# Seven block products for the first product of an expert, in a kernel of pooled attention and two mixtures of experts

## The chip, the core and the metric

The kernel runs on one core of one Trainium2 chip, as one program. The metric is the time of one execution on the device in microseconds (us), the median of several runs. A profile of one more execution gives the start and the length of every instruction on the engines: PE (TensorE; PEld is its weight load, which lies beside the matmuls), DVE (VectorE), ACT (ScalarE), POOL (GpSimd) and SP, which here only issues transfers. In the rows of the profile a name ending in q (SPq, PEq) is the engine's instruction sequencer.

## What is computed

An attention over keys and values that are pooled by eight, then a mixture of eight experts of which each token takes two, then a mixture of four experts that every token takes. There are 2304 tokens of 512 numbers; every expert is a product with a 512 by 1024 matrix, a ReLU and a product with a 1024 by 512 matrix. The two mixtures, cut to the core:

```python
for e in range(E):                      # 8 experts, the two best of a token
    for k in range(2):
        mask = top2[:, k] == e
        h = np.maximum(x[mask] @ w1[e], 0.0)
        out[mask] += top2_w[mask, k, None] * (h @ w2[e])
...
for e in range(E):                      # 4 experts, all of them
    h = np.maximum(x @ w1[e], 0.0)
    out += p[:, e:e + 1] * (h @ w2[e])
```

## The kernel before

**Attention and routing** take the first tenth of the time. Tokens stand on the partitions in 18 tiles of 128. Each tile's attention output goes to a DRAM tensor `x_d`; the routing (the generator `routing`, some 60 small DVE operations for a group of tiles, run a few at a time by `step`) turns the noisy logits into lists of tokens for each expert. An expert of the first mixture has 640 slots, that is 5 tiles.

**The first mixture** runs 16 chunks, two for each expert, of 384 and 256 slots. The rows of a chunk are fetched by POOL with an indirect DMA (`gather`, line 490), turned by four PE transposes each and split by ACT and DVE into a rounded part and a remainder (`turn`, lines 497 to 501), because every product is made of three float32r products: rounded times rounded, rounded times remainder, remainder times rounded. `layer1` makes 8 blocks of 128 hidden units for a chunk: 12 matmuls (4 blocks of the depth, 3 terms) into one PSUM bank, with the chunk's tokens as the 384 or 256 columns that stream by (line 593). ACT applies the ReLU (595) and DVE keeps the remainder (596). `layer2` makes 128 tokens by 512 outputs: 24 matmuls of 512 columns into one bank (607). The results go to a DRAM tensor `y_d`.

**The second mixture** takes 18 tiles as six chunks of 384 tokens. A token's two rows of `y_d` are fetched by POOL (`fetch2`), mixed (`mix2`), turned, and stay in SBUF for four experts; three chunks run through expert 0, 1, 2, 3, then the other three through 3, 2, 1, 0.

**The weights** come as 120 transfers of 512 KB (line 467), two blocks of 128 hidden units each. `w_split` rounds them on ACT (475) and takes the remainder on DVE (476); eight slots hold the result. In the attention phase and in the first chunk the remainder is taken by POOL instead, eight times.

**The order of the work** is written out by hand. Each engine runs its queue in the order in which the program text issues the instructions. `run_chunk` counts units (8 of `layer1`, then two for each tile of `layer2`), and `fills` says before which unit a fetch, a mix or a turn is issued. A conditional (line 718, between the last two chunks of the first mixture) holds a slow path for an overfull expert; it isn't taken here, but every engine reads its condition.

Of the kernel before, what the change touches and what calls it, by code (L numbers as in the profile page):

```python
# [29 lines left out]
CHUNKS = ((256, 384),) + ((384, 256),) * (E1 - 1)  # L30
CA = 384
# [9 lines left out]
WP, WP1 = 8, 6  # L41
# [4 lines left out]
def tile_attention_moe_moe(  # L46
# [256 lines left out]
    nc.gpsimd.memset(least[:, 0:1], float(CHUNKS[0][0]))  # L303
# [3 lines left out]
    def routing(g, hold):  # L307
# [99 lines left out]
        if g == EARLY - 1 or last:  # L407
            slots[last] = consts.tile([128, HC], I32, name=f"slots{int(last)}")
            nc.vector.tensor_copy(slots[last], slotf)
            fetch1(int(last))  # L410
            yield
# [38 lines left out]
    seq = [(wa, e) for e in range(E1)]  # L450
    seq += [(wb, e) for e in range(E2)]
    seq += [(wb, e) for e in range(E2 - 2, -1, -1)]
    n_pairs = 8 * len(seq)
    w_sl = [None] * WP
    for i in range(WP1):
        w_sl[i] = wts1.tile([128, 2, 2, 512], FR, name=f"w{i}")
    w_st = {}
    w_at = {"load": 0, "split": 0, "used": 0}

    def w_load():  # L460
        s = w_at["load"]
        if s < n_pairs:
            x, p = divmod(s, 8)
            src, e = seq[x]
            w_st[s] = stg.tile([128, 2, 512], FT, name="w_st")
            j = p % 4
            nc.sync.dma_start(w_st[s], src[e, p // 4][:, 2 * j:2 * j + 2])
            w_at["load"] += 1

    def w_split(eng=None):  # L470
        s = w_at["split"]
        if s >= min(n_pairs, w_at["used"] + WP):
# [7 lines left out]
    def w_get(x, m, f, part):  # L480
        s = 8 * x + 4 * m + f // 2
        assert w_at["used"] <= s < w_at["split"], (x, m, f, w_at)
        return w_sl[s % WP][:, f % 2, part]


    gat, mid, xt = {}, [], []

    def gather(key, src, n, idx):
        g = mid[0].tile([128, DM], FT, name="gat", bufs=6)
# [4 lines left out]
    def turn(src, dst, c):  # L494
# [3 lines left out]
        p3 = p.rearrange("p (k c) -> p k c", c=128)  # L498
        hi = dst[:, 0, :, c * 128:(c + 1) * 128]
        nc.scalar.activation(hi, p3, AF.Copy)  # L500
        nc.vector.tensor_sub(dst[:, 1, :, c * 128:(c + 1) * 128], p3, hi.bitcast(FT))  # L501

    def fetch1(ci):
# [299 lines left out]
```

## Time and profile before

| | before |
|---|---|
| median of three runs | 1390.43 us (1389.38 to 1391.59) |
| the profiled execution | 1388.02 us, of which the span of the instructions is 1386.2 us |
| granted TensorE clock, mean | 0.988 of full speed |
| PE busy | 1358.1 us, 98% of the span |
| DVE, ACT, POOL busy | 504.2, 392.4, 132.3 us |
| DMA | 118.33 MB, a mean of 85 GB/s |

A row of the list by shape names the source line, the engine, the operation, the output and inputs, and then the number of instructions and their busy time; the mean length of a matmul there holds the time until its result has left the array, so that consecutive matmuls overlap, and the spacing of a stream is read from the starts in the timeline. In the list of stretches the columns are the stretch, its length, then for PE, PEld, DVE, ACT and POOL the busy time and the number of instructions, the granted clock, the DMA share and GB/s.

### The profile page before, as it was taken

The numbers are of one execution on the slowest core, as the hardware profiler recorded it, in microseconds if no ns is written. First come the engines' busy times: TensorE is split into PE (matmuls) and PEld (weight loads), VectorE is DVE, ScalarE is ACT, GpSimd is POOL, SyncE is SP. The second block draws the span as 40 slices with busy tenths as digits, with TensorE's granted clock in tenths as the row PEclk, the third lists the DMA queues.
The fourth block names the chain that finished last, engine by engine and source line by source line (L and its number), as shares of the span: only waits on it lengthen the run. The fifth ranks groups of instructions, "written<-read, shape, count | busy, mean of one in ns | idle before, by whom it ended". The sixth has DMA issues, their size and how long they took to land.

```text
span 1386.2 us, 18129 instructions
## 1 busy us (share of the span) xinstructions
PE 1358.1 (98%) x7511; PEld 1238.0 (89%) x7511; DVE 504.2 (36%) x958; ACT 392.4 (28%) x759; POOL 132.3 (10%) x130
## 2 busy tenths in 40 slices
PE   7888999999999999999999999999999999999998
PEld 6787899998999989899999999999999999999997
DVE  6886324342243422433322432323213313313311
ACT  6752334343343433422211222212212212212211
POOL 6422200010000000331000010001000000000000
PEclk9988999999999999999999999999999999999999
DMA  9542423243232422441210310202001101102000
GB/s 369 192 137 64 157 99 124 101 157 114 100 124 99 150 91 85 149 134 46 79 43 16 97 56 31 91 24 69 24 0 58 64 0 61 62 0 61 31 30 24
DMA packets 37896, 118.33 MB, mean 85 GB/s; under 512 B 4784, under 2 KB 6064, under 8 KB 36656
## 3 DMA queue, kind: packets, MB, share of 16 engines
q1 hardware_dynamic: 31728, 97.18, 20.6%
q0 software_dynamic: 6080, 19.93, 4.6%
q8 instruction: 61, 1.00, 0.3%
q14 instruction: 27, 0.22, 0.0%
HBM read 97.17 MB, written 19.92 MB: 84 GB/s over the span
## 4 chain that ended last, share of the span: by engine, by line
PE 59%; issue 0%; ACT 0%; DVE 0%
PE p L593 30%; PE p L607 29%; PE tr L497 1%; DVE acc L738 0%; ACT yo L639 0%; ACT xt L500 0%
## 5 line engine op out<-in xcount | busy, mean ns | idle before, releaser
L593 PE MATMUL p<-xt,w 128*128 128x384 f32 (+1 forms) x3840 | 643.9, 326 | 2.2 <-ACT xt L500 1.5
L593 PEld LDWEIGHTS p<-xt,w 128*128 128x128 f32 x3840 | 631.4, 190 | 6.2 <-ACT xt L500 1.9
L607 PE MATMUL p<-w,hs 128*128 128x512 f32 x2688 | 624.5, 391 | 0.0
L607 PEld LDWEIGHTS p<-w,hs 128*128 128x128 f32 x2688 | 501.7, 188 | 102.2
L595 ACT ACTIVATE hs<-p 128x384 fp32r<-128x384 f32 (+1 forms) x320 | 150.6, 470 | 686.2 <-PE p L593 684.2
L596 DVE SCALAR_TENSOR_TENSOR hs<-p,hs 128x384 fp32r<-128x384 f32 (+1 forms) x320 | 169.0, 529 | 479.4 <-ACT hs L595 479.2
L476 DVE TENSOR_TENSOR w<-w_st,w 128x1024 fp32r<-128x1024 f32 x112 | 137.2, 1225 | 49.0 <-ACT w L475 49.0
L475 ACT ACTIVATE w<-w_st 128x1024 fp32r<-128x1024 f32 x120 | 126.5, 1054 | 1.4 <-DMA w_st<-wb 1.3
L738 DVE SCALAR_TENSOR_TENSOR acc<-p,pe,acc 128x512 f32<-128x512 f32 x54 | 40.6, 751 | 225.7 <-PE p L607 225.7
L490 POOL DMA_INDIRECT gat<-y_d,rows x36 | 41.8, 1160 | 432.8 <-ACT x L653 325.0
L639 ACT ACTIVATE yo<-p 128x512 f32<-128x512 f32 x40 | 23.9, 598 | 172.5 <-PE p L607 167.3
L490 POOL DMA_INDIRECT gat<-x_d,slots x40 | 39.7, 993 | 331.1 <-PE tr L497 285.6
L500 ACT ACTIVATE xt<-tr 128x512 fp32r<-128x512 f32 x58 | 34.4, 596 | 79.1 <-PE tr L497 78.8
L501 DVE TENSOR_TENSOR xt<-tr,xt 128x512 fp32r<-128x512 f32 x58 | 39.9, 689 | 32.7 <-ACT xt L500 32.6
L269 PE MATMUL pv<-va,et 128*128 128x81 f32 (+1 forms) x320 | 40.5, 286 | 5.2 <-DVE lgm L283 5.2
L269 PEld LDWEIGHTS pv<-va,et 128*128 128x128 f32 (+1 forms) x320 | 38.1, 201 | 6.9 <-issue 5.5
L736 DVE TENSOR_SCALAR acc<-p,pe 128x512 f32<-128x512 f32 x18 | 13.5, 751 | 68.7 <-PE p L607 68.7
L231 PE MATMUL s<-kb,q_sb 128*128 128x144 f32 (+1 forms) x160 | 27.9, 319 | 5.8 <-DMA q_sb<-qt 3.1
L231 PEld LDWEIGHTS s<-kb,q_sb 128*128 128x128 f32 (+1 forms) x160 | 21.1, 193 | 8.3 <-issue 4.0
L248 ACT ACTIVATE es<-s,mx 128x72 f32<-128x72 f32 x108 | 25.5, 320 | 10.0 <-DVE mx L238 6.8
L497 PE MATMUL tr<-ident,gat 128*128 128x128 f32 x160 | 24.6, 280 | 1.0 <-DVE xt L501 1.0
L262 ACT ACTIVATE et<-et 72x512 f32<-72x512 f32 x36 | 21.4, 594 | 7.8 <-PE et L260 7.5
(105 smaller groups left out, 320.0 us busy)
## 6 DMA issues: line engine op xcount, KB each, us to landing
w_st<-wa SPq DMA_DIRECT2D x64, 512.0 KB, 4.5
w_st<-wb SPq DMA_DIRECT2D x56, 512.0 KB, 3.9
y_d<-yo SPq DMA_DIRECT2D x40, 256.0 KB, 2.0
x_d<-xs SPq DMA_DIRECT2D x18, 256.0 KB, 4.2
out<-acc SPq DMA_DIRECT2D x18, 256.0 KB, 2.0
k_st<-kt SPq DMA_DIRECT2D x3, 1152.0 KB, 11.4
v_st<-vt SPq DMA_DIRECT2D x3, 1152.0 KB, 11.7
q_sb<-qt SPq DMA_DIRECT2D x3, 1152.0 KB, 14.2
```

Of the source, the lines that this page charges most:

```text
L231: nc.tensor.matmul(p[r0:r1, h * 144:(h + 1) * 144], q_sb[b][:, hp, a0:a1], kb[:, b, hp, :], start=True, stop=True)
L269: nc.tensor.matmul(p[r0:r1, h * VW:(h + 1) * VW], ets[i][:, h * 128 + r0:h * 128 + r1], va[:, b * H + 4 * g + h, :], start=True, stop=True)
L475: nc.scalar.activation(w[:, :, 0], w_st[s], AF.Copy)
L476: (eng or nc.vector).tensor_sub(w[:, :, 1], w_st[s], w[:, :, 0].bitcast(FT))
L490: nc.gpsimd.indirect_dma_start(out=g, out_offset=None, in_=src[0:n, :], in_offset=bass.IndirectOffsetOnAxis(ap=idx, axis=0))
L497: nc.tensor.transpose(p[:, kd * 128:(kd + 1) * 128], src[:, kd * 128:(kd + 1) * 128], ident)
L501: nc.vector.tensor_sub(dst[:, 1, :, c * 128:(c + 1) * 128], p3, hi.bitcast(FT))
L593: nc.tensor.matmul(p, w[:, kd], xs[:, b, kd, :n], start=i == 0, stop=i == 3 * KD - 1)
L595: nc.scalar.activation(hs[:, 0, f, :n], p, AF.Relu)
L596: nc.vector.scalar_tensor_tensor(hs[:, 1, f, :n], p, 0.0, hs[:, 0, f, :n].bitcast(FT), op0=OP.max, op1=OP.subtract)
L607: nc.tensor.matmul(p, hs[:, a, f, t * 128:(t + 1) * 128], w_get(x, 1, f, b), start=f == 0 and i == 0, stop=f == FB - 1 and i == 2)
L738: nc.vector.scalar_tensor_tensor(a, p, w, a, op0=OP.mult, op1=OP.add)
```

## The change

**First product.** Where a chunk is large enough, the product of its tokens with a pair of hidden blocks is made in 2 by 2 blocks (two halves of the tokens by two halves of the depth, two halves of the depth by two hidden blocks) with seven block products and 15 additions instead of eight products (Strassen's scheme in Winograd's form). Each block product has 6 matmuls (2 blocks of the depth, 3 terms). Six experts of the first mixture run so, with all 640 slots as one chunk, hence 320 columns; and in the second mixture the tokens go as three chunks of 768, hence 384 columns, through four experts each, but for the first expert of the first chunk. That one and the first and last experts of the first mixture stay in the plain form (`run_plain`), in pieces of 256 or 384 tokens.

**Sums.** Four sums of token blocks are made by DVE once for a chunk (`sums`), and the seven operands are rounded by ACT (`x_hi`) and their remainders taken by DVE (`x_lo`). Four sums of weight blocks are made by POOL for each pair (`parts_of`, lines 505 to 508), rounded by ACT in two operations (510, 512), with the remainders by POOL in two (514, 516). All other weights (499, 501) have their remainders taken by POOL as well. Of the additions on the products, one is a copy by ACT (725) and five are by DVE on PSUM (728 to 747); two use the accumulation of a bank that already holds an earlier product.

**Halves and rings.** An expert runs in two halves of 512 hidden units: `layer1` or `layer1_seven` for two pairs, then `layer2` with 12 matmuls for each tile, whose two halves are added by ACT and DVE outside PSUM. The weights are 184 transfers of 512 KB, four to a half (two pairs of the first product, two of the second), in two rings of three slots. Tables say at which unit of a half each step of the weights is issued (`SEVEN_AHEAD`, `ahead_plain`); in it item 3 is the second pair of the second product of the same half, items 4 and 5 the pairs of the next half's first product, and item 6 the first of the next half's second. The buffers of the fetched rows are 4 instead of 6.

```diff
--- before.py
+++ after.py
-CHUNKS = ((256, 384),) + ((384, 256),) * (E1 - 1)
-CA = 384
+FIRST = 256
+CA, CW = 384, 768
...
-WP, WP1 = 8, 6
+
+CHUNK_KINDS = [(0, 0, False)] * 2 + [(0, e, True) for e in range(1, E1 - 1)] + [(0, E1 - 1, False)] * 2
+CHUNK_KINDS += [(1, 0, False)] * 2 + [(1, e, True) for e in range(1, E2)] + [(1, e, True) for e in range(E2)] * 2
+
+A11, S2, S3, S1, A12, A22, S4 = range(7)
+B11, B21, B22, T1, T2, T3, T4 = range(7)
...
+    items = []
+    for src, e, h, wino in halves:
+        items += [(src, e, 0, 2 * h, wino), (src, e, 0, 2 * h + 1, wino), (src, e, 1, 2 * h, False),
+                  (src, e, 1, 2 * h + 1, False)]
+    R1, R2 = 3, 3
+    w1r = [wts1.tile([128, 2, 7, 256], FR, name=f"u{i}") for i in range(R1)]
+    w2r = [wts1.tile([128, 2, 2, 512], FR, name=f"v{i}") for i in range(R2 - 1)]
...
+    def parts_of(s, eng):
+        st = w_st[s]
+        if not items[s][4]:
+            w = w_slot(s)
+            w = w[:, :, 0:4] if s % 4 < 2 else w.rearrange("p a f c -> p a (f c)").rearrange(
+                "p a (q c) -> p a q c", c=256)
+            nc.scalar.activation(w[:, 0], st, AF.Copy)
+            yield
+            eng.tensor_sub(w[:, 1], st, w[:, 0].bitcast(FT))
+        else:
+            w = w_slot(s)
+            t = comb[0]
+            nc.gpsimd.tensor_sub(t[:, 0], st[:, 0], st[:, 1])
+            nc.gpsimd.tensor_sub(t[:, 1], st[:, 3], t[:, 0])
+            nc.gpsimd.tensor_sub(t[:, 2], st[:, 3], st[:, 0])
+            nc.gpsimd.tensor_sub(t[:, 3], st[:, 2], t[:, 1])
+            yield
+            nc.scalar.activation(w[:, 0, 0:3], st[:, 1:4], AF.Copy)
+            yield
+            nc.scalar.activation(w[:, 0, 3:7], t, AF.Copy)
+            yield
+            nc.gpsimd.tensor_sub(w[:, 1, 0:3], st[:, 1:4], w[:, 0, 0:3].bitcast(FT))
+            yield
+            nc.gpsimd.tensor_sub(w[:, 1, 3:7], t, w[:, 0, 3:7].bitcast(FT))
-        w = w_sl[s % WP]
-        nc.scalar.activation(w[:, :, 0], w_st[s], AF.Copy)
-        (eng or nc.vector).tensor_sub(w[:, :, 1], w_st[s], w[:, :, 0].bitcast(FT))
-        w_at["split"] += 1
-        w_load()
...
     def gather(key, src, n, idx):
-        g = mid[0].tile([128, DM], FT, name="gat", bufs=6)
+        g = mid[0].tile([128, DM], FT, name="gat", bufs=4)
         nc.gpsimd.indirect_dma_start(out=g, out_offset=None, in_=src[0:n, :],
                                      in_offset=bass.IndirectOffsetOnAxis(ap=idx, axis=0))
...
+    def layer1_seven(q, pr, n, fills, u):
+
+        w = pair_weights(q, pr)
+        fa, fb = 2 * pr, 2 * pr + 1
+
+        def bank():
+            return pm.tile([128, 512], FT, name="wn", bufs=4)[:, :n]
+
+        def product(p, xm, wm, first=True):
+            i = 0
+            for a, b in TERMS:
+                for kd in range(2):
+                    nc.tensor.matmul(p, w[:, a, wm, kd * 128:(kd + 1) * 128], xc[xm][:, b, kd, :n],
+                                     start=first and i == 0, stop=i == 5, skip_group_check=True)
+                    i += 1
+
+        def go(i):
+            for f in fills.get(u + i, ()):
+                f()
+
+        p1, p6, p7, p5 = (bank() for _ in range(4))
+        s1, u2, u3 = (moe.tile([128, CA], FT, name=f"u{i}")[:, :n] for i in range(3))
+        go(0)
+        product(p1, A11, B11)
+        nc.scalar.activation(s1, p1, AF.Copy)
+        go(1)
+        product(p6, S2, T2)
+        nc.vector.tensor_add(u2, p6, s1)
+        go(2)
+        product(p7, S3, T3)
+        nc.vector.tensor_add(u3, p7, u2)
+        go(3)
+        product(p5, S1, T1)
+        nc.vector.tensor_add(p6, p5, u3)
+        lo22 = relu_split(fb, n, n, p6)
+        go(4)
+        product(p1, A12, B21, False)
+        lo11 = relu_split(fa, 0, n, p1)
+        lo22()
+        lo11()
+        go(5)
+        product(p7, A22, T4, False)
+        nc.vector.tensor_add(p7, p7, u2)
+        lo21 = relu_split(fa, n, n, p7)
+        go(6)
+        product(p5, S4, B22, False)
+        nc.vector.tensor_add(p5, p5, u2)
+        lo12 = relu_split(fb, 0, n, p5)
+        lo21()
...
+    def layer2(q, t):
+        p = pm.tile([128, 512], FT, name="p2", bufs=2)
+        for f in range(FB // 2):
+            s = 4 * q + 2 + f // 2
+            w_check(s)
+            w = w_slot(s)
+            for i, (a, b) in enumerate(TERMS):
+                nc.tensor.matmul(p, hs[:, a, f, t * 128:(t + 1) * 128], w[:, b, f % 2],
+                                 start=f == 0 and i == 0, stop=f == FB // 2 - 1 and i == 2)
         return p
...
+    def ahead_plain(q, u, last):
+
+        seven = 4 * q + 4 < len(items) and items[4 * q + 4][4]
+        if u == 0:
+            w_whole(4 * q + 3)
+        if not seven:
+            if u in (2, 4):
+                w_whole(4 * q + 3 + u // 2)
+            if u == last:
+                w_whole(4 * q + 6)
+        else:
+            for k, i, n in ((1, 4, 1), (2, 4, 1), (3, 4, 2), (4, 4, 9), (4, 5, 1), (5, 5, 2), (last, 5, 9),
+                            (last, 6, 9)):
+                if k == u:
+                    w_step(4 * q + i, n)
+
+    SEVEN_AHEAD = {0: (3, 1), 1: (3, 1), 2: (4, 1), 4: (4, 1), 7: (4, 1), 8: (4, 1), 9: (4, 1), 12: (5, 1),
+                   14: (5, 1), 15: (5, 2), 16: (5, 1), 17: (6, 1), 18: (6, 1)}
...
+    def run_seven(n, sink, fills):
+        subs = 2 * n // 128
+        for h in range(2):
+            q = at_half[0]
+            fl = {k[1]: list(f) for k, f in fills.items() if k[0] == h}
+            for u, (i, k) in SEVEN_AHEAD.items():
+                fl.setdefault(u, []).append(lambda i=i, k=k: w_step(4 * q + i, k))
+            for pr in range(2):
+                layer1_seven(q, pr, n, fl, 7 * pr)
+                w_at["used1"] += 1
+            for t in range(subs):
+                for f in fl.get(14 + t, ()):
+                    f()
+                step(3, 1)
+                sink(h, t, layer2(q, t))
+            w_at["used2"] += 2
+            at_half[0] += 1
...
+    def window(n):
+
+        for i, m in enumerate(ORDER):
+            add(1, 8 + i, x_hi, m, n)
+            add(1, (14, 14, 15, 16, 17, 17, 18)[i], x_lo, m, n)
...
+    for c in range(4):
+        add(0, 0, fetch1, 1, c)
+    for c in range(5):
+        add(*((0, 4), (0, 5), (0, 6), (1, 0), (1, 1))[c], turn_full, (1, c), c)
+        if c == 0:
+            add(0, 4, fetch1, 1, 4)
+    add(1, 2, sums, CS)
+    for i, m in enumerate(ORDER):
+        add(1, 3 + i // 2, x_both, m, CS)
+    run_plain(A22, S4, CA, sink1(0, FIRST), fills)
...
+            for c in range(4):
+                add(0, 0, fetch1, e + 1, c)
+            for c in range(5):
+                add(0, (8, 10, 12, 14, 17)[c], turn_full, (e + 1, c), c)
+                if c == 0:
+                    add(0, 8, fetch1, e + 1, 4)
+            add(0, 18, sums, CS)
+            window(CS)
...
+    with tc.If(nc.values_load(over[0:1, 0:1], min_val=0, max_val=1) != 0):
+        all_experts()
+    for t in range(2):
+        add(0, 0, fetch2, t)
+        add(0, 5, mix2, t)
+        add(1, 0, turn2, t, (A11, A12), t)
+    add(1, 0, fetch2, 2)
+    add(1, 4, mix2, 2)
+    add(1, 5, turn2, 2, (A11, A12), 2)
+    run_plain(S3, S4, CAP - CA, sink1(e, CA), fills)
...
+    add(0, 1, sums, CA)
+    add(0, 4, x_both, S2, CA)
+    add(0, 5, x_both, S3, CA)
+    add(0, 6, x_both, S4, CA)
+    add(1, 4, x_both, S1, CA)
+    run_plain(S1, A22, CA, sink2(0, accs, 3, True, False), fills)
```

The order of instructions moves at three places that matter below. First POOL's queue around the conditional. In these rows gat is a fetched tile, y_d the DRAM result of the first mixture, w_st a staged weight transfer, u and v slots of the rings of the first and of the second product, comb the sums of weight blocks. Before:

```order
L476 TENSOR_TENSOR w_1556<-w_st,w_1556 128x2x512
L490 DMA gat<-x_d,slots_1853 128x512 x38
L718 TENSOR_LOAD over
L718 COMPARE_AND_BRANCH
...
L718 UNCONDITIONAL_BRANCH x2
L490 DMA gat<-y_d,rows 128x512 x36
```

Now, from the branch on:

```order
L955 UNCONDITIONAL_BRANCH x2
L540 DMA gat<-y_d,rows 128x512 x4
L501 TENSOR_TENSOR v_167<-w_st,v_167 128x1024
L501 TENSOR_TENSOR u_165<-w_st,u_165 128x1024
L501 TENSOR_TENSOR u_163<-w_st,u_163 128x1024
L501 TENSOR_TENSOR v_last<-w_st,v_last 128x1024
L540 DMA gat<-y_d,rows 128x512 x2
L501 TENSOR_TENSOR v_166<-w_st,v_166 128x1024
```

The fetches had the queue to themselves; now the first four stand ahead of the remainder of slot v_167, which the same half's second product reads.

Second, POOL's queue at the passage from the plain to the seven-product form in the second mixture (the end of the last plain half, then the start of the next):

```order
L505 TENSOR_TENSOR comb<-w_st 128x256
L506 TENSOR_TENSOR comb<-w_st,comb 128x256
L507 TENSOR_TENSOR comb<-w_st 128x256
L508 TENSOR_TENSOR comb<-w_st,comb 128x256
L514 TENSOR_TENSOR u_164<-w_st,u_164 128x768
L516 TENSOR_TENSOR u_164<-comb,u_164 128x1024
L501 TENSOR_TENSOR v_166<-w_st,v_166 128x1024
L540 DMA gat<-y_d,rows 128x512 x4
L501 TENSOR_TENSOR v_167<-w_st,v_167 128x1024
L505 TENSOR_TENSOR comb<-w_st 128x256
L506 TENSOR_TENSOR comb<-w_st,comb 128x256
```

Before, POOL held only fetches there; now the weight sums of the next half come behind two pairs, four fetches and a remainder.

Third, ACT's queue in a half of 320 columns. Before, a rounding of weights (L475) stood between two ReLUs (L595):

```order
L595 ACTIVATE hs<-p_3546 128x384
L475 ACTIVATE w_167<-w_st 128x2x512
L595 ACTIVATE hs<-p_3565 128x384
L475 ACTIVATE w_168<-w_st 128x2x512
L595 ACTIVATE hs<-p_3584 128x384
```

Now (L679 is the ReLU, L725 the copy of the first product, xf the turned tokens):

```order
L725 ACTIVATE u_2779<-wn 128x320
L679 ACTIVATE hs<-wn 128x320
L510 ACTIVATE u_165<-w_st 128x768
L679 ACTIVATE hs<-wn 128x320 x3
L512 ACTIVATE u_165<-comb 128x1024
L725 ACTIVATE u_2859<-wn 128x320
L567 ACTIVATE xf<-tr 128x4x128 x2
L679 ACTIVATE hs<-wn 128x320 x2
```

The rounding that reads POOL's sums (L512) stands directly ahead of the copy on which the second pair's additions depend.

## Rows read from the trace of the kernel before

**Rows 1.** The page's first part: busy time, share of the span, instructions of each engine.
```profile
PE 1358.1 (98%) x7511; PEld 1238.0 (89%) x7511; DVE 504.2 (36%) x958; ACT 392.4 (28%) x759; POOL 132.3 (10%) x130
```
**Rows 2.** Waits of PE: engine, line, waited for: us in total, times, longest.
```profile
PE p L593 <- ACT xt L500: 1.5, 2, 0.8
```
**Rows 3.** Timeline of PE: start, length, line, operation, count of the streams.
```profile
193.92 16.52 PE L607 MATMUL p<-w,hs 128*128 128x512 f32 x72
210.28 5.91 PE L593 MATMUL p<-xt,w 128*128 128x256 f32 x48
...
557.53 11.74 PE L593 MATMUL p<-xt,w 128*128 128x256 f32 x96 [0.64 <-PEq L718]
569.11 5.63 PE L607 MATMUL p<-w,hs 128*128 128x512 f32 x24
...
616.92 16.83 PE L593 MATMUL p<-xt,w 128*128 128x384 f32 x96
633.58 5.64 PE L607 MATMUL p<-w,hs 128*128 128x512 f32 x24
```
**Rows 4.** Instructions by line and shape, matmuls of the experts.
```profile
L607 PE MATMUL p<-w,hs 128*128 128x512 f32 x2688 | 624.5, 391 | 0.0
L593 PE MATMUL p<-xt,w 128*128 128x384 f32 x3072 | 543.0, 335 | 1.5 <-ACT xt L500 1.5
...
L593 PE MATMUL p<-xt,w 128*128 128x256 f32 x768 | 100.8, 292 | 0.8 <-PEq L718 0.6
```
**Rows 5.** Instructions by line and shape, the other engines: busy us, mean ns.
```profile
L596 DVE SCALAR_TENSOR_TENSOR hs<-p,hs 128x384 fp32r<-128x384 f32 x256 | 142.2, 556 | 339.3 <-ACT hs L595 339.2
L476 DVE TENSOR_TENSOR w<-w_st,w 128x1024 fp32r<-128x1024 f32 x112 | 137.2, 1225 | 49.0 <-ACT w L475 49.0
L475 ACT ACTIVATE w<-w_st 128x1024 fp32r<-128x1024 f32 x120 | 126.5, 1054 | 1.4 <-DMA w_st<-wb 1.3
L595 ACT ACTIVATE hs<-p 128x384 fp32r<-128x384 f32 x256 | 126.0, 492 | 634.8 <-PE p L593 634.8
...
L596 DVE SCALAR_TENSOR_TENSOR hs<-p,hs 128x256 fp32r<-128x256 f32 x64 | 26.8, 421 | 140.1 <-ACT hs L595 140.0
...
L595 ACT ACTIVATE hs<-p 128x256 fp32r<-128x256 f32 x64 | 24.6, 384 | 51.5 <-PE p L593 49.4
...
L476 POOL TENSOR_TENSOR w<-w_st,w 128x1024 fp32r<-128x1024 f32 x8 | 18.8, 2360 | 35.4 <-ACT w L475 35.4
...
L195 POOL TENSOR_TENSOR vp<-v_st 128x288 f32<-128x288 f32 x3 | 2.1, 713 | 0.2
```
**Rows 6.** Timeline of POOL behind the conditional: the first and the fourth fetch.
```profile
562.77 1.31 POOL L490 DMA_INDIRECT gat<-y_d,rows  x1 [87.58 <-SPq L718]
...
567.26 0.95 POOL L490 DMA_INDIRECT gat<-y_d,rows  x1 [0.30 <-issue]
```
**Rows 7.** Transfers by line: count, KB each, median us from issue to landing.
```profile
w_st<-wb SPq DMA_DIRECT2D x56, 512.0 KB, 3.9
...
gat<-y_d,rows POOLq DMA_INDIRECT x36, 3.7
```
**Rows 8.** Timeline of POOL and of DVE in the attention phase, and one line's DVE instructions.
```profile
71.62 2.36 POOL L476 TENSOR_TENSOR w<-w_st,w 128x1024 fp32r<-128x1024 f32 x1 [3.38 <-ACT w L475]
...
72.83 1.17 DVE L412 SCALAR_TENSOR_TENSOR rows<-ei,g_pf 128x8 int32<-128x8 f32 x1
...
121.93 0.16 DVE L412 SCALAR_TENSOR_TENSOR rows<-ei,g_pf 128x6 int32<-128x6 f32 x1
...
L280 DVE TENSOR_TENSOR xs<-pv,rec x36: 401/424/426, 21.2 to 103.4; 128x256 f32<-128x256 f32 x36
```
**Rows 9.** Stretches around a stop of PE, and a stream of PE at the lower clock.
```profile
88.00:92.00 4.00, 1.23 (x11) 0.99 (x10) 3.90 (x18) 1.42 (x5) 0.00 (x0) 1.00 0.62 176
92.00:96.00 4.00, 3.39 (x29) 3.20 (x29) 2.83 (x13) 1.42 (x5) 0.00 (x0) 0.64 0.23 87
...
118.10 8.50 PE L593 MATMUL p<-xt,w 128*128 128x256 f32 x48
```

More of the change, by code (lines that the diff above doesn't have):

```diff
@@ L409, in routing @@
             nc.vector.tensor_copy(slots[last], slotf)
-            fetch1(int(last))
+            for c in range(3 if last else 2):
+                fetch1(0, 2 + c if last else c, not last)
             yield
@@ L447, in warm @@
                              start=True, stop=True)
[L450 to L458, printed above, removed]
+    halves = []
+    for k in CHUNK_KINDS:
+        src, e, wino = k[0], k[1], k[2]
+        for h in range(2):
+            halves.append(((wa, wb)[src], e, h, wino))
@@ L488, in gather, with w_step, w_whole, w_check @@
+    def w_step(s, n=1, eng=None):
+        if s >= len(items):
+            return
+        if s not in w_parts:
+            w_parts[s] = parts_of(s, eng or nc.gpsimd)
+        for _ in range(n):
+            if next(w_parts[s], 0) == 0:
+                return
+    def w_whole(s, eng=None):
+        w_step(s, 9, eng)
+    def w_check(s):
+        assert s in w_parts and next(w_parts[s], 0) == 0, s
+    gat, mid, xc, xf, sx = {}, [], {}, [], []
     def gather(key, src, n, idx):
-        g = mid[0].tile([128, DM], FT, name="gat", bufs=6)
+        g = mid[0].tile([128, DM], FT, name="gat", bufs=4)
@@ L611, in run_chunk @@
-    def run_chunk(x, xs, n, last, sink, fills, rate=3, lo=None):
-        units = FB + n // 64
-        for u in range(units):
-            for f in fills.get(u, ()):
-                f()
-            step(rate, 1)
-            if u < FB:
-                layer1(x, xs, n, u)
-                if last and u % 2:
-                    w_at["used"] += 1
-            else:
-                t, half = divmod(u - FB, 2)
-                p = layer2(x, t, half)
-                if half:
-                    sink(t, p)
-            w_split(lo)
-        if last:
-            w_at["used"] += 4
-        for f in fills.get(units, ()):
-            f()
+        relu_split(f, 0, n, p)()
@@ L744, in tile_attention_moe_moe @@
[L744 to L757 removed]
+    fills = {}
@@ new lines, in add @@
+    def add(h, u, f, *a):
+        fills.setdefault((h, u), []).append(lambda: f(*a))
+    ORDER = (A11, S2, S3, S1, A12, A22, S4)
+    CS = CAP // 2
+    def window(n):
+        for i, m in enumerate(ORDER):
+            add(1, 8 + i, x_hi, m, n)
+            add(1, (14, 14, 15, 16, 17, 17, 18)[i], x_lo, m, n)
+    add(1, 4, until, lambda: True in slots)
+    fills["end"] = [lambda c=c: turn_plain((0, 2 + c), (A22, S4), c) for c in range(3)]
+    run_plain(S1, S2, FIRST, sink1(0, 0), fills, 14)
```

320 lines of the change are left out of this document (193 added, 127 removed).

## The prediction

> **What bounds the kernel now.** I read the busy times first: PE is busy 98% of the span, every other engine 36% or less [rows 1]. Then PE's waits: in the experts the only repeated one is 1.5 us in all, for a turned chunk [rows 2]. Then the timeline of PE, to see what a matmul costs in a stream, which the listed mean length doesn't tell: 96 matmuls of 384 columns take 616.92 to 633.58, so 173.5 ns each; 96 of 256 columns 557.53 to 569.11, so 120.6 ns; 72 of 512 columns 193.92 to 210.28, so 227.2 ns [rows 3]. The three lie on one line, columns at 2.4 GHz plus about 14 ns, and each has its own weight load. PE's stream is therefore the time; DVE, ACT and POOL cost nothing as long as they stay ahead.
>
> **PE's saving.** Before there are 3072 matmuls of 384 and 768 of 256 columns [rows 4]: 3072 x 173.5 + 768 x 120.6 = 625.6 us. After, a chunk in seven products has 4 pairs x 7 x 6 = 168 matmuls where two plain chunks of that width have 192. Six chunks of 320 columns give 1008, eleven of 384 columns 1848; the plain chunks give 384 of 384 and 192 of 256 columns. The price at 320 columns isn't shown; it lies between 120.6 and 173.5 ns, and since both neighbours lie on the line I take the middle, 147.1. That is 2232 x 173.5 + 1008 x 147.1 + 192 x 120.6 = 558.7 us: **66.9 us less**. The ends of that bound move the sum by 27 us either way. The second product keeps its 2688 matmuls of 512 columns, the turns their number.
>
> [...]
>
> **What the seven-product halves ask of the others.** A half lasts 84 x 173.5 + 72 x 227.2 ns = 30.9 us (384 columns) or 84 x 147.1 + 60 x 227.2 ns = 26.0 us (320). For a pair, DVE has 5 additions and 4 remainders, at about the 556 ns of a remainder [rows 5] 5.0 us of PE's 7.3. ACT has five operations at 492 ns and the two roundings, 0.8 and 1.05 us: 4.3. POOL is new: a remainder of 1024 columns takes it 2.36 us, an addition of 288 columns 0.71 [rows 5], so a pair in sums costs 4 x 0.71 + 0.75 x 2.36 + 2.36 = 7.0 us, and a half 2 x 7.0 + 2 x 2.36 = 18.7 us. All three fit. The order decides, then. The weight rounding that reads POOL's sums stands ahead of the copy of the second pair's first product. I follow POOL in a steady half of 320 columns: remainder of item 3 at 4.2 us, sums at 7.0; ACT comes to them at 7.5. So it holds, by half a microsecond, and 1.1 us more go before PE's fifth product waits for that copy. At 384 columns the margin is over 3 us.
>
> Two small waits stay there. Between the pairs PE's next product needs the bank that the chain addition, ReLU, weight rounding (0.8 us), ReLU, remainder frees: 2.8 us against 2.65 for three products at 320 columns, so 0.17 us in 12 halves, 2 us; none at 384. And where the next chunk's operands are prepared, DVE holds up a bank of the second product by some 1.7 us, in the two chunks of 384 columns: 3.4 us. **Together 5.4 us** (0 to 15).
>
> **Behind the conditional.** POOL's first fetch came 5.2 us after PE's first matmul there, the fourth 9.7 us after it and was issued at 10.7 [rows 6]. Now the remainder of item 3 is queued behind these four: done at 10.7 + 2.36 = 13.1 us. PE wants it in the second product of the same half, after 48 x 0.1206 + 7 x 0.2272 = 7.4 us: 5.7 us of waiting. The transfer of a later item is issued when that remainder is done and lands 3.9 us later [rows 7]; ACT waits for it ahead of its ReLUs, and the third tile's fetch lands 3.7 us after its issue [rows 7], behind two more remainders. I carry this to the end of the chunk and get 7.6 us in all. In the next chunk the fetches wait for the last stores and stand ahead of item 3 again: 1.7 us. **9.3 us** (nothing, if POOL's fetches come before the branch's release, to 16).
>
> **From plain to seven products, second mixture.** The last plain half of 16.5 us holds two pairs in sums and two other remainders, 18.7 us for POOL, ending some 3.8 us late. Then come four fetches (5.8 us), a remainder and the sums: 14.8 us into the half, where ACT asks at 8.5. Copy done at 16.2, PE's fifth product wanted it at 11.5: **4.7 us** (0 to 8).
>
> **The same passage in the first mixture** would cost 4.2 us in this way. But it also has DVE's four sums and seven remainders in the same half. A DVE operation on small SBUF tiles that takes 0.16 us elsewhere took 1.17 us and ended with POOL's operation, which had begun before it: 72.83 + 1.17 against 71.62 + 2.36. The 36 operations on one PSUM and one SBUF input never took over 426 ns, whatever POOL did [rows 8]. So sums and operand remainders, with two SBUF inputs, will wait for POOL by up to 2.36 us each and hold it up by their own 0.8 us; followed operation by operation the passage then costs 11 us. The steady additions on PSUM don't. Between 4.2 and 11 I take **7.6 us**, since only those operations that meet a running POOL operation wait.
>
> [...]
>
> **First chunk.** The same contention delays the routing's small operations: four remainders on POOL where two were; PE waits for the lists. 0 to 4.7 us, I take **2.5**.
>
> **Clock.** When PE was busy 1.2 us of 4, the granted clock fell to half in the stretch behind it; 48 matmuls at the low clock took 8.50 us where they take 5.91 [rows 3, 9]. A stop of that size costs 2.6 us more. The terms hold three (behind the conditional and at both passages): **7.8 us** (0 to 13).
>
> **Sum.** 1388.0 (profiled execution; its span is 1386.2) - 66.9 + 5.4 + 9.3 + 4.7 + 7.6 + 2.5 + 7.8 = 1358.4 us. That execution is 2.4 us below the median of the runs shown, so I forecast **1361 us**.
>
> **Rivals.** (1) *Everything is hidden.* The tables put each step of the weights a half ahead, and the terms of the passages rest on queues that I followed by hand, each with a few microseconds of possible slack. For it: POOL's load is below the half's length on the mean. Against it: behind the conditional the order leaves no way round. The time is 1388.0 - 66.9 + 5.4 + 2.4 = 1329 us. Chance 0.20.
> (2) *DVE queues behind POOL in every chunk, and the kernel gets slower.* In seven chunks DVE makes four sums and seven remainders for the next one while POOL works 18.7 us of each half. In those two halves DVE has about 10 us to spare. At a mean wait of 0.8 us, which I get from the three long POOL operations that fall there, nothing shows. Each 0.1 us more over the 11 operations is 7.7 us in all, and from a mean of 1.3 us the kernel is slower than before; at 1.4 us it takes 1361 + 7 x (11 x 1.4 - 10) = 1399 us. For it: the 1.17 us of [rows 8]; against it: DVE, once first, holds POOL as well. Chance 0.10.
> (3) *The change doesn't do what it says:* matmuls of 320 columns cost as much as those of 384, 1361 + 1008 x 0.0264 = 1388 us, no change. Against it: 256 columns go faster, with the same weight load each. Chance 0.03.
>
> **How the numbers follow.** The forecast's own case, 1340 to 1384 us by the bounds above, has 0.64; 0.03 is left for other accidents. The range 1328 to 1384 takes in the first rival and leaves out the others. A measurement of this kernel tells 0.2% (2.8 us) from no change. Faster: 0.64 + 0.20 + 0.03 = 0.87; the same 0.03; slower 0.10.
>
> **What would show it.** Right: streams of 320 columns at 147 ns, 3432 matmuls of the first product where there are 3840 now; PE waits of over 4 us behind the conditional and at both passages, and hardly any in the seven-product halves; DVE sums and remainders of up to 3 us where POOL runs. Wrong: no such waits (rival 1), or PE waiting in every chunk's second product for a bank (rival 2).

## The result, and the profile after

The changed kernel takes **1368.92 us** (median of four runs, 1366.58 to 1371.64) against 1389.91 us (1389.35 to 1391.59) for the kernel before on the same chip: a ratio of 0.9848 (95% interval 0.9827 to 0.9868), 21 us faster. The forecast was 1361 us, faster. The profiled execution took 1368.53 us, 19.5 us less than the one of before, where the sum had 29.6 us.

The first part of the page, beside [rows 1]:

```profile
PE 1306.1 (96%) x7103; PEld 1175.1 (86%) x7103; DVE 736.2 (54%) x1368; ACT 570.3 (42%) x1041; POOL 887.3 (65%) x646
```

PE has 408 matmuls less and is busy 52 us less; POOL went from 10% to 65%. The waits of PE in the experts, where [rows 2] had one row of 1.5 us (us in total, times, longest; some rows between belong to the attention):

```profile
PE p L759 <- POOL v_last L501: 7.1, 1, 7.1
PE tr L552 <- DVE gat L847: 6.5, 4, 2.8
PE wn L713 <- ACT u L725: 5.7, 2, 4.0
PE p L759 <- DVE hs L680: 4.4, 2, 3.4
...
PE wn L696 <- PEq L955: 2.8, 1, 2.8
...
PE p L759 <- POOL v L501: 1.8, 1, 1.8
PE tr L552 <- DMA gat<-x_d,slots: 1.6, 2, 1.2
...
PE p L759 <- DVE acc L976: 1.1, 2, 0.5
```

In these rows wn is a bank of the first product, p one of the second, hs the hidden values, x an operand, tr a turned tile and acc a sum of results. All have counts of 1 to 4: these are waits of single places, not of the repeated halves. The streams of PE's timeline that answer to [rows 3], then the two passages from the plain form to seven products, and then the places behind the conditional:

```profile
219.63 12.48 PE L713 MATMUL wn<-x,u 128*128 128x320 f32 x84
231.94 0.39 PE L759 MATMUL p<-v,hs 128*128 128x512 f32 x1
...
705.22 14.75 PE L713 MATMUL wn<-x,u 128*128 128x384 f32 x84
719.80 1.55 PE L759 MATMUL p<-v_last,hs 128*128 128x512 f32 x6
```

```profile
177.74 1.61 PE L759 MATMUL p<-v,hs 128*128 128x512 f32 x3 [3.43 <-DVE hs L680]
180.29 7.99 PE L759 MATMUL p<-v,hs 128*128 128x512 f32 x25 [0.94 <-DVE hs L680]
...
667.38 11.63 PE L713 MATMUL wn<-x,u 128*128 128x384 f32 x66
683.02 4.93 PE L713 MATMUL wn<-x,u 128*128 128x384 f32 x18 [4.01 <-ACT u L725]
```

```profile
553.36 7.46 PE L696 MATMUL wn<-x,u 128*128 128x256 f32 x48 [2.78 <-PEq L955]
560.65 1.78 PE L759 MATMUL p<-v,hs 128*128 128x512 f32 x7
564.22 4.16 PE L759 MATMUL p<-v,hs 128*128 128x512 f32 x17 [1.79 <-POOL v L501]
569.57 0.63 PE L552 MATMUL tr<-ident,gat 128*128 128x128 f32 x4 [1.18 <-DVE gat L847]
572.32 0.63 PE L552 MATMUL tr<-ident,gat 128*128 128x128 f32 x4 [2.13 <-DVE gat L847]
...
585.98 8.51 PE L696 MATMUL wn<-x,u 128*128 128x384 f32 x48
594.33 1.55 PE L759 MATMUL p<-v,hs 128*128 128x512 f32 x6
595.72 0.39 PE L759 MATMUL p<-v_last,hs 128*128 128x512 f32 x1
603.25 2.50 PE L759 MATMUL p<-v_last,hs 128*128 128x512 f32 x5 [7.14 <-POOL v_last L501]
608.51 1.09 PE L552 MATMUL tr<-ident,gat 128*128 128x128 f32 x4 [2.76 <-DVE gat L847]
```

84 matmuls of 320 columns take 219.63 to 231.94, 146.5 ns each; 84 of 384 take 173.6 ns. So the saving is there, almost to the microsecond. But behind the conditional PE stops six times in 55 us, and the worst stop, 7.14 us, is in the chunk from 585.98 on, where I had put 1.7 us. POOL, DVE and SP there:

```profile
586.19 2.40 POOL L501 TENSOR_TENSOR v<-w_st,v 128x1024 fp32r<-128x1024 f32 x1 [1.49 <-ACT v L499]
596.12 0.96 POOL L540 DMA_INDIRECT gat<-y_d,rows  x1 [7.53 <-issue]
...
599.88 0.94 POOL L540 DMA_INDIRECT gat<-y_d,rows  x1 [0.30 <-issue]
600.84 2.35 POOL L501 TENSOR_TENSOR v_last<-w_st,v_last 128x1024 fp32r<-128x1024 f32 x1
603.14 4.66 POOL L501 TENSOR_TENSOR u<-w_st,u 128x1024 fp32r<-128x1024 f32 x2
...
600.98 7.38 DVE L847 SCALAR_TENSOR_TENSOR gat<-gat,wt 128x512 f32<-128x512 f32 x1 [5.31 <-DMA gat<-y_d,rows]
...
588.62 0.33 SPq L483 DMA_DIRECT2D w_st<-wb  x1
588.99 0.42 SPq L837 DMA_DIRECT2D y_d<-acc  x1
```

These read as follows. The last store to `y_d` is issued at 588.99 only, behind a weight load that waits for a staging buffer, which POOL's remainder frees at 588.6. The fetches need that store and begin at 596.12, 10.1 us after the chunk's first matmul: 3.0 us until the store is issued and 7.1 us from there to the first fetch. In the kernel before, the same two points were 581.8 and 584.63, 2.8 us apart. So the longer part of the delay lies behind the issue. The trace's DMA packets show the store's last one ending 5.6 us after the issue, where a load of 512 KB had been issued 0.4 us ahead on the same queue and its packets run until 5.0 us; in the kernel before, with no load near, the store's last packet ended after 1.6 us. No run moves that load alone. The remainder of item 3 stands behind the four fetches. The mixing on DVE (two SBUF inputs) begins at 600.98 and ends at 608.36, just after the last of three remainders on POOL. It takes 0.75 us where POOL is still (experiment 2).

### The profile page after: what moved, and what is told of

It reads as the page before. It is cut to its first block, busy times and chain, and to the rows that moved or that the text cites. A ratio compares the mean times of both kernels' runs of the same rounds, so it can differ in the third digit from the quotient of the medians.

```text
span 1366.8 us, 18815 instructions
## 1 busy us (share of the span) xinstructions
PE 1306.1 (96%) x7103; PEld 1175.1 (86%) x7103; DVE 736.2 (54%) x1368; ACT 570.3 (42%) x1041; POOL 887.3 (65%) x646
## 4 chain that ended last, share of the span: by engine, by line
PE 50%; DVE 3%; POOL 3%; issue 2%; DMA 1%; ACT 1%; SPq 0%; POOLq 0%; DVEq 0%; ACTq 0%
PE p L759 26%; PE wn L713 22%; DVE x L592 1%; PE wn L696 1%; DVE gat L847 1%; POOL v L501 1%; PE tr L552 1%; DVE acc L976 0%; DMA y_d<-acc 0%; POOL gat L540 0%; POOL v_last L501 0%; DVE sx L581 0%; ACT hs L679 0%; DVE hs L680 0%; DMA w_st<-wb 0%
## 5 line engine op out<-in xcount | busy, mean ns | idle before, releaser
L713 PE MATMUL wn<-x,u 128*128 128x384 f32 (+1 forms) x2856 | 479.9, 327 | 5.7 <-ACT u L725 5.7
L713 PEld LDWEIGHTS wn<-x,u 128*128 128x128 f32 x2856 | 471.8, 188 | 9.0 <-ACT u L725 6.3
L759 PE MATMUL p<-v,hs 128*128 128x512 f32 x1812 | 448.3, 394 | 6.7 <-DVE hs L680 4.4
L759 PEld LDWEIGHTS p<-v,hs 128*128 128x128 f32 x1812 | 339.7, 189 | 79.4 <-DVE hs L680 6.5
L679 ACT ACTIVATE hs<-wn 128x384 fp32r<-128x384 f32 (+2 forms) x320 | 147.1, 469 | 301.2 <-DVE wn L734 150.2
L501 POOL TENSOR_TENSOR v<-w_st,v 128x1024 fp32r<-128x1024 f32 x62 | 154.6, 2495 | 139.0 <-ACT v L499 138.9
L680 DVE SCALAR_TENSOR_TENSOR hs<-wn,hs 128x384 fp32r<-128x384 f32 (+2 forms) x320 | 163.6, 528 | 146.1 <-ACT hs L679 134.4
L759 PE MATMUL p<-v_last,hs 128*128 128x512 f32 x876 | 227.7, 395 | 7.8 <-POOL v_last L501 7.1
L759 PEld LDWEIGHTS p<-v_last,hs 128*128 128x128 f32 x876 | 164.5, 189 | 43.9 <-POOL v_last L501 7.6
L516 POOL TENSOR_TENSOR u<-comb,u 128x1024 fp32r<-128x1024 f32 x68 | 168.7, 2480 | 34.5 <-ACT u L512 33.9
L696 PE MATMUL wn<-x,u 128*128 128x384 f32 (+1 forms) x576 | 99.5, 335 | 3.5 <-PEq L955 2.8
L696 PEld LDWEIGHTS wn<-x,u 128*128 128x128 f32 x576 | 96.7, 206 | 5.0 <-issue 3.2
L512 ACT ACTIVATE u<-comb 128x1024 fp32r<-128x1024 f32 x68 | 71.6, 1053 | 20.5 <-POOL comb L508 20.5
```

The lines of the kernel that those rows point to most:

```text
L501: eng.tensor_sub(w[:, 1], st, w[:, 0].bitcast(FT))
L512: nc.scalar.activation(w[:, 0, 3:7], t, AF.Copy)
L516: nc.gpsimd.tensor_sub(w[:, 1, 3:7], t, w[:, 0, 3:7].bitcast(FT))
L679: nc.scalar.activation(hi, p, AF.Relu)
L680: return lambda: nc.vector.scalar_tensor_tensor(hs[:, 1, f, c0:c0 + n], p, 0.0, hi.bitcast(FT), op0=OP.max, op1=OP.subtract)
L696: nc.tensor.matmul(p, w[:, a, qu, (kd % 2) * 128:(kd % 2 + 1) * 128], xc[(xa, xb)[kd // 2]][:, b, kd % 2, :n], start=i == 0, stop=i == 11)
```

## Experiments

**1. The remainder ahead of the fetches** (in the two chunks behind the conditional).

```diff
+                if rest_first and u == 0:
+                    ahead_plain(q, u, FB // 2 + n // 128 - 1)
                 for f in fl.get(u, ()):
                     f()
```

> The one edit: in the last 256 columns of the first mixture and in the first plain chunk of the second, POOL's remainder of item 3 is queued ahead of the four fetches instead of behind them. Theory A (my step behind the conditional: the remainder standing behind the fetches is the whole price): both of PE's waits for POOL, 1.79 and 7.14 us, go and nothing takes their place; with some 2 us of clock, 1357 us. Theory B: in the chunk behind, the fetches themselves are late (issued 10 us after PE's first matmul there, since the last store to y_d stands on SP behind a weight load) and the mixing on DVE is drawn out by POOL (8.0 us for two operations); then PE stops at the turn for the mixed tile instead: 7.14 goes, 2.76 grows to 6 or more, 1.79 goes and 1.2 + 2.1 grow by some 2 us; 1363 to 1366 us. I hold B likelier.

1364.87 us, ratio 0.9819 (0.9801 to 0.9836). PE's waits for POOL are gone, and the waits for the mixed tile went from 6.5 to 12.2 us (waits of PE):

```profile
PE tr L552 <- DVE gat L850: 12.2, 4, 6.3
```

So theory B: the order of that one remainder is worth about 4 us (the two intervals overlap at their ends; in the profiled executions it is 4.1 us); the late fetches and the drawn-out mixing stand close behind it.

**2. DVE takes the plain remainders** from the end of the first mixture to the passage in the second.

```diff
+        eng = nc.vector if 18 <= q <= 23 else None
...
-            w_whole(4 * q + 3)
+            w_whole(4 * q + 3, eng)
```

> The plain remainders of the weights that are issued in the plain halves from the end of the first mixture on (256 columns behind the conditional, and the two plain chunks of the second mixture) go to DVE instead of POOL, about 1.05 to 1.2 us each there for 2.4 us on POOL. Theory (POOL's queue and its contention with DVE make the waits): PE's waits for POOL (1.79, 7.14) go, the mixing operations fall from a mean of 4 us to 0.75 us, the store to y_d is no longer held up by a late weight load so the fetches of the next chunk come 2 to 3 us earlier, and the wait for ACT's copy in the passage to seven products (4.01) shrinks to under 1 us because POOL starts that half 4.8 us earlier; 1351 us (1346 to 1357). Rival (DVE becomes the late one): the remainder of the hidden tile queues behind a weight remainder, PE's second product waits for it several times by 0.5 to 1.2 us, and the time stays above 1362 us.

1353.95 us, ratio 0.9731 (0.9715 to 0.9747), 15 us less than the change. From the timeline of DVE:

```profile
563.18 1.22 DVE L501 TENSOR_TENSOR u<-w_st,u 128x1024 fp32r<-128x1024 f32 x1 [0.52 <-ACT u L499]
...
568.69 0.75 DVE L848 SCALAR_TENSOR_TENSOR gat<-gat,wt 128x512 f32<-128x512 f32 x1 [1.40 <-ACT gat L847]
570.50 0.75 DVE L848 SCALAR_TENSOR_TENSOR gat<-gat,wt 128x512 f32<-128x512 f32 x1 [1.07 <-ACT gat L847]
```

A remainder takes 1.22 us where POOL took 2.4, and the mixing its bare 0.75. PE has no wait for POOL left; for the mixed tile 4.2 us in all (6.5 in the change), 3.4 of it in the second chunk, where the first fetch is issued at 592.39, still 8.6 us after the chunk's first matmul: 1.5 us earlier, not the 2 to 3 us of the theory, and still 6.6 us after the store's issue. The copy in the passage is waited for by 2.49 us instead of 4.01, more than the under 1 us of the theory.

**3. The fetches behind the sums** in the first seven-product half of the second mixture.

```diff
-                    add(0 if t < c else 0, 0 if t < c else 16, fetch2, t)
+                    add(0, (0 if k or sc else 3) if t < c else 16, fetch2, t)
```

> In the first seven-product half of the second mixture the four fetches move from ahead of unit 0 to ahead of unit 3, behind item 3's remainder and the four sums on POOL. Theory (the chain of my step: POOL's fetches hold the sums, the sums hold ACT's rounding, the rounding holds the copy that PE's eleventh product needs): the wait of 4.01 us goes entirely, and with it 1.6 us of low clock behind it: 1363 us. Rival (the copy is late for ACT's own queue, or POOL is late anyway by what it carries over from the plain half): at least 2 us of the wait stay, 1366 to 1368 us.

1363.55 us, ratio 0.9799 (0.9782 to 0.9816). The 84 matmuls that were broken after 66 now run without a stop (timeline of PE), and a turn waits 1.59 us instead:

```profile
667.67 14.75 PE L713 MATMUL wn<-x,u 128*128 128x384 f32 x84
682.26 2.92 PE L759 MATMUL p<-v,hs 128*128 128x512 f32 x12
686.77 0.63 PE L552 MATMUL tr<-ident,gat 128*128 128x128 f32 x4 [1.59 <-DVE gat L847]
```

The chain of queues that the step followed (fetches, sums, rounding, copy, product) is the cause: with the fetches moved, the 4.01 us are gone.

**4. POOL's weight operations on 16 of 256 columns.**

```diff
-            eng.tensor_sub(w[:, 1], st, w[:, 0].bitcast(FT))
+            eng.tensor_sub(w[:, 1, :, :TW], st[:, :, :TW], w[:, 0, :, :TW].bitcast(FT))
...
-            nc.gpsimd.tensor_sub(t[:, 0], st[:, 0], st[:, 1])
+            nc.gpsimd.tensor_sub(t[:, 0, :TW], st[:, 0, :TW], st[:, 1, :TW])
```

> POOL's sums and remainders of the weights (and the plain remainders) cover 16 of each 256 columns only, the rest of the second parts stays zero: the output is left without most of the correction terms. Fetches, order and PE's work stay. It prices everything that POOL's length and its contention with DVE cost. Theory: the waits for POOL (8.9 us), for ACT's copy (5.7), for the hidden tile's remainder at the first passage (4.4), the mixing (6.5, of which some 3 stay since the fetches behind the conditional still wait for the last store) and some 5 us of low clock go: 1341 us (1336 to 1347); DVE's sums and operand remainders fall to their bare length, 0.7 to 1.3 us at 640 columns, each as regular as those on PSUM. Rival (the waits come from the order of the queues, not from POOL's durations): 1358 us or more, with the waits at the same places.

1337.25 us (one run). The tiles are cleared by DVE at the start, which delays the second chunk by 3.7 us; from that chunk's first long stream to the end of the span it takes 35 us less than the change. That is what POOL's length costs, by its own time and by what it does to DVE; this run doesn't part the two. Both passages have no wait at all. The waits that stay (3.2 and 1.9 us for POOL behind the conditional) are those of order: the remainder still stands behind the fetches. One line's operand remainders and the third sum on DVE in the steady halves, first in the kernel after and then here (lengths: least, median, most, in ns):

```profile
L592 DVE TENSOR_TENSOR x<-xf,x x20: 811/1346/2416, 234.4 to 461.5; 128x640 fp32r<-128x640 f32 x20
...
L581 DVE TENSOR_TENSOR xf<-xf x4: 3018/3018/3022, 271.0 to 434.0; 128x640 f32<-128x640 f32 x4
```

```profile
L595 DVE TENSOR_TENSOR x<-xf,x x20: 815/818/891, 227.6 to 452.3; 128x640 fp32r<-128x640 f32 x20
...
L584 DVE TENSOR_TENSOR xf<-xf x5: 947/948/949, 209.8 to 427.1; 128x640 f32<-128x640 f32 x5
```

The same operation takes 0.82 us when POOL works briefly and up to 2.4 us when it doesn't.

**5. Operand remainders made twice**, the test of rival 2.

```diff
-            add(1, (14, 14, 15, 16, 17, 17, 18)[i], x_lo, m, n)
+            for _ in range(2):
+                add(1, (14, 14, 15, 16, 17, 17, 18)[i], x_lo, m, n)
```

> Each of the seven operand remainders on DVE that prepare the next chunk is made twice, in the seven chunks that have such a window: 10 us more of DVE per chunk, where the two inputs lie in SBUF and meet POOL. It tests the price of rival 2. The trace after shows a mean wait of 0.58 us over the 11 operations of a chunk (the third sum 3.02 us for 0.82 bare, the remainders 1.42 for 0.82); doubling adds what 0.9 us more of mean wait would. My price (DVE has some 10 us to spare over the two halves of a chunk): 3.6 us of that are left, so 7 x 6.4 = 45 us more, 1413 us. Second theory (the half in which they stand has nothing to spare, and DVE can't catch up without PE waiting): the whole 10 us each time and low clock behind, 1440 us or more, PE waiting for banks of the second product and for chain additions. Third (DVE catches up in the next half): under 1385 us.

1422.13 us (one run): 53 us more than the change, 7.6 us for each window, between the first and the second theory. PE now waits for banks of the second product (waits of PE), in the change 1.1 us in all:

```profile
PE p L759 <- DVE acc L835: 21.0, 5, 4.2
PE p L759 <- DVE acc L977: 9.8, 3, 4.8
```

A DVE that is kept too long does make PE wait, as rival 2 had it, and in this form the kernel is slower than before. The operand remainders keep DVE busy 149 us where it was 89 in the change, some 9 us more for each window. PE's waits for these banks and for the chain additions grew by 32.5 us, 4.6 for each window, so about 4 us of the 9 were to spare: my price was 3.6. What it left out is the clock: behind the long waits PE's next matmuls take 1.7 to 2.6 us more than their price in each window. By a straight line between the two points, an estimate, the kernel would be as slow as before at a mean wait of some 0.9 us, where I had put 1.3; the change has 0.58.

**6 to 8. The branch.** PE's wait at the conditional grew from 0.64 us to 2.78, which no step had. Its sequencer's branch instruction took longer, and the DMA engines were busier. In the edit, `held_loads` counts the loads that would be issued from there on, and they are issued behind the conditional.

```diff
             if u == last:
+                if q == 17:
+                    held_loads[0] = 0
                 w_whole(4 * q + 6)
```

> One weight load of 512 KB that SP issues in the last 2 us ahead of the conditional is issued behind it instead. Theory: PE's branch takes 3.85 us where the DMA engines are 6% busy (before), 4.36 at some 50% (tiny POOL), 6.2 to 6.5 us where they are 92% busy (after, and two experiments), so what it waits for comes through the DMA engines behind that load: the branch falls to under 5 us and PE's wait there from 2.8 to under 1.6 us; 1366 to 1368 us in all. Rival (it waits for the slowest engine's part of the branch, DVE's or SP's): the wait stays within 0.3 us of 2.8.

1370.59 us (one run), the wait 3.3 us, the branch 6.7 us. The forecast failed; but the load ahead of it was still on its way, and the DMA engines were still 65% busy during the branch. So all loads of that half were held back from unit 2 on:

> Three weight loads (1.5 MB) that SP issues in the second half of the plain chunk ahead of the conditional are issued behind it, so that only the three stores of 256 KB remain on the DMA engines there. Theory (PE's branch waits for something that comes through the DMA engines behind the loads): the branch falls from 6.2 us to under 5 us and PE's wait from 2.8 to under 1.6 us; the late loads then cost more behind it than this gains. Rival (it waits for DVE's or SP's part of the branch, which come 0.7 and 2.0 us after PE's last matmul): the wait stays within 0.3 us of 2.8.

and in the kernel before, two idle copies were put there:

```diff
+            if e == E1 - 1 and c0 == 0 and t == 1:
+                for i in range(2):
+                    nc.sync.dma_start(spare[i * 128:(i + 1) * 128, :],
+                                      wb[0, 0][:, 2 * i:2 * i + 2].rearrange("p f c -> p (f c)"))
```

> The kernel before with two idle copies of 512 KB from DRAM to DRAM that SP issues behind the second last store ahead of the conditional; nothing reads them. There PE's branch took 3.85 us and PE's wait 0.64 us with the DMA engines 6% busy. Theory (busy DMA engines draw out the branch): 6 us or more and a wait of over 2 us. Rival (the copies don't matter, the order of DVE and SP does): 3.85 us and 0.64 us again, within 0.3.

Here is the branch instruction of PE's sequencer (length in ns, start in us) in the kernel before, in the kernel after, in the kernel after with the loads held back, and in the kernel before with the copies:

```profile
L718 PEldq COMPARE_BRANCH  x1: 3845/3845/3845, 553.5 to 553.5; - x1
```

```profile
L955 PEldq COMPARE_BRANCH  x1: 6235/6235/6235, 547.0 to 547.0; - x1
```

```profile
L962 PEldq COMPARE_BRANCH  x1: 3575/3575/3575, 546.3 to 546.3; - x1
```

```profile
L723 PEldq COMPARE_BRANCH  x1: 5988/5988/5988, 555.5 to 555.5; - x1
```

With the DMA engines 6%, 84%, 28% and 76% busy during it, PE waits 0.64, 2.78, 1.33 and 2.78 us; the two edited kernels take 1366.62 and 1392.57 us (one run each). In both directions it goes with the transfers. The rival is out: with the loads held back PE's branch ends at 549.9, ahead of DVE's (550.4) and SP's (551.8), so it waits for neither. What it waits for stands in the DMA packets of the traces. In each of the twelve kernels one packet of 16 KB of the queue that the page calls instruction begins during PE's branch, and the branch ends 1.39 to 1.42 us after that packet, whatever its length. The packet begins 1.1 to 1.5 us after the branch's start in the three kernels with quiet DMA engines (before, with POOL's short operations, with the loads held back) and 3.6 to 4.4 us after it in the nine others. So the branch waits for a fetch of instructions, and in these kernels busy DMA engines make that fetch late.

**9, 10. Together.** Experiments 2, 3 and the first form of 6, with the mixing and the turns behind the conditional in the second half of their chunks, and the first mixture's passage with later fetches:

```diff
-        add(0, 5, mix2, t)
-        add(1, 0, turn2, t, (A11, A12), t)
-    add(1, 0, fetch2, 2)
+        add(1, 1, mix2, t)
+        add(1, 3 + t, turn2, t, (A11, A12), t)
+    add(1, 2, fetch2, 2)
...
-                add(0, 0, fetch1, e + 1, c)
+                add(0, 3 if e == 1 else 0, fetch1, e + 1, c)
...
```

> Together: plain remainders on DVE from the end of the first mixture on, the fetches of the second mixture's first seven-product half behind the sums, the mixing and turns behind the conditional moved from the first to the second half of their chunks (where the fetched tiles have long landed), the weight load behind the conditional, and in the first seven-product half of the first mixture fetches at unit 3 with turns at units 13 to 18. Theory (each wait was found at its cause, and nothing else stands close behind it): the 3.4 + 0.8 us for the mixed tile, the 2.5 and 1.9 us for ACT's copy, 1.5 us of the branch and some 4 us of low clock go from 1354 us: 1342 us (1338 to 1347). Rival (the late fetches take other work with them: a later turn collides with the second product's banks): above 1348 us.

1344.30 us, ratio 0.9664 (0.9648 to 0.9680). It lies in the forecast range and, with the next version, which the runs don't tell from it, is the fastest that computes everything, 25 us under the change. The 1.5 us hoped for at the branch were not gained: the wait there is 2.9 us. The waits that are left (waits of PE):

```profile
PE p L764 <- DVE hs L685: 4.4, 2, 3.4
...
PE tr L557 <- DVE gat L855: 3.2, 2, 3.0
...
PE wn L701 <- PEq L963: 2.9, 1, 2.9
```

The last version moves DVE's work at the first mixture's passage behind the hidden tile:

```diff
-    add(1, 2, sums, CS)
+    add(1, 2, sums, CS, (0, 1))
+    add(1, 4, sums, CS, (2, 3))
     for i, m in enumerate(ORDER):
-        add(1, 3 + i // 2, x_both, m, CS)
+        add(1, (3, 4, 5, 5, 6, 6, 6)[i], x_both, m, CS)
```

> As the combination before, and at the first mixture's passage the third and fourth sum and the operand remainders from S2 on stand two units later on DVE, behind the last hidden tile's remainder, instead of ahead of it. Theory (the 3.5 + 0.9 us wait for the hidden tile's remainder is the order on DVE, sums ahead of it): the wait goes, with 3 us of low clock; DVE, which is full there, hands some 2 to 3 us on to the next half as waits for the operands S1 and A12: 1338 us. Rival (DVE's length there, drawn out by POOL, is what PE waits for, wherever it stands): the same time as the combination without it, within 2 us.

1345.73 us, ratio 0.9689 (0.9672 to 0.9706), the same as the combination before. PE's timeline shows the wait in its two new places:

```profile
180.77 4.60 PE L764 MATMUL p<-v,hs 128*128 128x512 f32 x12 [2.38 <-DVE acc L843]
...
192.63 3.87 PE L718 MATMUL wn<-x,u 128*128 128x320 f32 x24 [2.87 <-DVE u L736]
```

So the rival holds there: DVE is full from 169 to 192 us, and by experiment 4, where this passage has no wait, it is POOL that fills it.

## Why the prediction was right, and where its sum was off

The sign and the mechanism held. In the terms, low clock is what the matmuls took above the price of their stream in the five stretches behind the first chunk where the granted clock was 0.50 to 0.52 of full speed (48 matmuls of 256 columns in 7.29 us for 5.79, 18 of 384 in 4.77 for 3.12). The first chunk is taken with its own low clock, by the end of the first stream of the chunk behind it (153.48 us for 150.30):

| term, us | predicted | the trace after |
|---|---|---|
| PE's saving | -66.9 | -67.5 (146.5 ns at 320 columns for 147.1) |
| small waits of the steady halves | +5.4 | +1.1 (two of 0.5) |
| first chunk | +2.5 | +3.2 |
| passage, first mixture | +7.6 | +7.2 (3.43, 0.94, 1.15, 1.72) |
| behind the conditional, same chunk | +7.6 | +5.1 (1.79, 1.18, 2.13) |
| the chunk after it | +1.7 | +10.4 (7.14, 2.76, 0.45) |
| the branch itself | none | +2.1 |
| passage, second mixture | +4.7 | +4.0 |
| low clock | +7.8 | about +10.5 |
| sum | -29.6 | -23.9; measured -19.5 |

Some 4 us stay unassigned.

- **PE's saving.** Right, by the line through the two neighbours: it gave 147.1 ns at 320 columns, the trace has 146.5.
- **Behind the conditional.** The step that failed is the second half of it, "in the next chunk the fetches wait for the last stores and stand ahead of item 3 again: 1.7 us". The mechanism is the one named, the size is not. I had taken the fetches to come as before, 2.3 us after the chunk's first matmul. With two halves to a chunk the last store comes at the chunk's end, and it stands on SP behind a load that POOL holds up, so it was issued 3.0 us after that matmul; then 7.1 us passed to the first fetch, where it had been 2.8 us before. So the fetches came at 10.1 us. The store's packets ran beside those of the load ahead of it; no run tests that apart. And I had given the mixing its bare length, though it has two SBUF inputs as the operations of [rows 8]. Experiments 1 and 2 show both parts: with the order alone repaired 4 us come back, with POOL still 15 (in which the passage behind it has a part).
- **Passages.** Both waits came at the passages, and experiments 3 and 4 show the causes. That 7.2 meets 7.6 in the first mixture is partly luck: the wait for the copy is 1.72 us, where the queues had given 4.2, and 1.15 us are for a fetched tile, which no step had. There the contention doesn't make PE wait for an operand, as I had it, but for the hidden tile's remainder, queued behind two sums of 2.47 and 2.98 us (0.82 each in experiment 4).
- **Contention.** The third sum takes 0.82 to 0.95 us beside POOL's short operations and 3.02 beside its long ones, and POOL is held as well: its remainder beside one such sum (270.99) took 2.94 us, for a median of 2.40. The additions on PSUM stay at 0.49 to 0.50 us (320 columns, means). The passage followed operation by operation, 11 us, was further off than the middle, 7.6: it came to 7.2, of which 4.4 are waits that the contention made.
- **Rival 1** (everything hidden, 1329 us) is what experiment 4 comes near; the change misses it by POOL's length. **Rival 2** is real, but the mean wait is 0.58 us for the 0.8 I took; its decision point lay nearer than I thought, since the price left out the low clock behind each wait. **Rival 3** is out.
- **Small waits.** No wait between pairs appears: 84 matmuls of 320 columns run without a stop, so the 0.17 us that I had worked out were not there. The bank of the second product held PE up by 0.5 us where I had 1.7.
- **First chunk.** The size is near, but no run tests the cause that I gave for it.
- **Clock.** Five stretches, not three; the extra ones are in the second half behind the branch and in the chunk that I had undersized. They cost 1.5 to 3.1 us each, where I took 2.6 from a stream of 8.50 us that ran at the lower level in part only (in the kernel before, the granted clock is 0.52 from 120 to 124 us and 1.00 behind).

## What to carry to other kernels

When work goes to an engine that was idle, look first not at its mean load but at the places where its queue holds something else that others need at a fixed time (a fetch behind a conditional, the first half after a change of form), and follow what a late store or load does there. Here DVE operations with two SBUF inputs grew beside POOL's long ones, from 0.82 to as much as 3.02 us, and those on PSUM didn't (0.49 to 0.50 us at 320 columns); so price the first kind by what runs beside it, above all where it stands ahead of a matmul. Where few places hold the loss, look there: of the some 47 us that the change lost of its saving, the moves of experiment 9 together gave back 25.

## What was not expected of the hardware

- The branch of PE's sequencer took 3.6 to 4.4 us with the DMA engines 6 to 49% busy (three kernels) and 6.0 to 6.7 us with them 63 to 84% busy (nine kernels); PE waited 0.6 to 1.3 us in the one case and 2.8 to 3.6 in the other. Each time it ended 1.4 us after a 16 KB packet of instructions, and that packet began later where the DMA engines were busy.
- A DVE operation of 0.75 us was kept from ending through three POOL operations on end, 7.38 us: in this one place it wasn't let in between them.
- A stop of PE of nearly the same length didn't cost the same clock. Behind the 2.78 us at the branch the granted clock was 0.75 from 553.3 to 560.0 in the kernel after, and 1.00 from 553.8 to 560.0 behind 2.90 us in the combined version. Why isn't shown.
